# All eight pairs of weight tiles in Strassen's scheme, and a new order of work, in an attention and feed-forward kernel on one core

## The chip, the core and the metric

The program runs on one core of a Trainium2 chip, in one launch. The metric is the device time of that launch in microseconds (us), smaller being better. TensorE (PE) multiplies matrices, VectorE (DVE), ScalarE (ACT) and GpSimd (POOL) do elementwise work, SyncE (SP) issues the transfers. All five run side by side and wait for one another through semaphores; each works through its own list in order.

## The reference

Attention with positive random features for 8 batches of 8 heads (576 tokens, 64 channels a head, 128 features), and then a feed-forward layer on the 4,608 tokens x 512 channels that it gives:

```python
q_p, k_p = phi(q_s), phi(k_s)          # exp features, 128 a head
kv = einsum('bhsm,bhsd->bhmd', k_p, v)
num = einsum('bhsm,bhmd->bhsd', q_p, kv)
den = einsum('bhsm,bhm->bhs', q_p, k_p.sum(2))[..., None] + 1e-06
x = (num / den) as 4608 tokens x 512
h = x @ w_in                           # 512 -> 2048
g = maximum(h, 0) + log1p(exp(-abs(h)))
out = g @ w_out                        # 2048 -> 512
```

## The kernel before

**The arithmetic.** Each fp32 number is kept as a high part (fp32r, cut by a copy) and a low part (the rest, by a subtraction), and each product of the two layers is three matmuls: high x high, high x low, low x high. The weights are 16 tiles of 128 hidden columns (`fc` 0 to 15). Layer 1 of one tile on 512 tokens is 4 channel blocks x 3 = 12 matmuls of 128x512, made in two halves of six. Layer 2 of one tile is four steps (`tt` 0 to 3, 128 tokens each) of three matmuls, added up over the 16 tiles in an `acc` bank of PSUM. Between the two stands softplus: Abs, Exp and Ln on ACT, a max and add on DVE, a high copy on ACT or DVE, a low subtraction on DVE or POOL.

**The blocks.** Tokens go in two blocks of 256 and eight of 512. The last 64 tokens of each batch (the "rest") have no place in their batch's block: they are saved to DRAM as they come (`plan_save`), and together they are the last block, t8, loaded back by `plan_rest` in two transfers. The block before it is t7. Both are made together in `plan_both`.

**Strassen's scheme.** `plan_both` multiplies t7 and t8 by the weights in pairs of tiles (fa, fb). For a pair that is a product of 2x2 blocks: two token blocks, two halves of the channels, two weight tiles; done plainly, eight products of six matmuls (`plan_plain`). `plan_pair` makes it in seven products `p1` to `p7` of six matmuls, from sums of weight blocks (128x256; nine sums, and the cutting of four of them into high and low parts) and sums of token blocks (128x512, `plan_sums`, once for each of two channel blocks c, for all pairs), and adds the products up with five operations on DVE. `PLAIN = 1` makes the first pair plainly and seven by the scheme. With `plan_sums` the sum `first` takes the place of t8's own first half of the channels in `xh`, `xl`, so it waits for the plain pair (`plains`).

**The order.** Nothing is scheduled when the kernel is built: all steps are put in a list of works, and `ORDER` is a written-out list of them (entry = 2 x number of the work + which of its engines makes it). Each engine gets its works in that order. `in_order` gives each work a buffer when its turn comes (`take`, the one that came free earliest) and returns it (`give`) at its last use; a work waits for the last user of its buffer. `timed` reckons the times again, and `with_fill` puts idle matmuls (`fill`, L1775) where it reckons a gap of PE that is long enough.

**Names below.** "xp" is the product that gives x for a part of a batch (`plan_x`, L1183); "l1" and "l2" are steps of layers 1 and 2 of the block before t7; "L2" those of t7 and then t8; "P1.p5" is product 5 of pair 1.

Of the kernel before, what the change touches and what calls it, by code (L numbers as in the profile page):

```python
# [11 lines left out]
F32R = mybir.dt.float32r  # L12
# [25 lines left out]
COLD, LAG = 2.6, 1.85  # L38
# [5 lines left out]
PLAIN = 1  # L44
# [418 lines left out]
def favor_softplus_kernel(ctx, tc, q0, k0, qx, kx, tx, vv, om, wi, wo, out):  # L463
# [894 lines left out]
    def plan_both(i, box):  # L1358
# [84 lines left out]
        def plan_sums(c):  # L1443
# [5 lines left out]
            def third(i):  # L1449
                for k in range(3 if not i else 0):  # L1450
                    b[k] = at.tile([P, 2, n], F32R, name=f"x{k + 2}_{c}", tag=b["s", k], bufs=1)
                    b["f", k] = temp(b["t", k], n, f"xf{k}_{c}")
# [432 lines left out]
```

## Time and profile before

| | |
|---|---|
| time, median of 3 runs (from, to) | 977.64 us (977.54 to 988.13) |
| the profiled execution: its own time | 976.84 us |
| its span, first to last instruction | 975.1 us |
| busy: PE, DVE, ACT, POOL | 964.5, 790.5, 675.5, 283.9 us |
| PE matmuls | 5,511 |
| chain that ended last, by engine | PE 92%, DVE 5%, ACT 2%, issue 1%, DMA 1% |
| granted clock of PE | 1.0 |

The span is what the profiler sees between the first and the last instruction; the rest of the time lies around it. A matmul's duration is modelled and longer than its step: 128x512 matmuls show some 390 ns and follow each other every 0.23 us. So the busy time of PE hides gaps under about 0.16 us, and a stall is read from the distance of two starts.

### The profile page before, as it was taken

How to read it: one execution, taken by the hardware profiler on the slowest of the kernel's cores; microseconds unless marked ns; L12 is line 12 of the kernel's file. 1: busy time of each engine (PE TensorE's matmuls, PEld its weight loads, DVE VectorE, ACT ScalarE, POOL GpSimd, SP SyncE). 2: the span in 40 equal slices, each digit the busy share in tenths (PEclk: the TensorE clock that was granted, in tenths of full speed). 3: DMA queues.
4: the chain of work that ended last, by engine and by line, in shares of the span. 5: the costliest groups of instructions: out<-in, count | busy, mean ns of one | idle time of the engine just before them, and what ended most of it. 6: DMA issues, size and time to landing. Idle time of an engine off the chain costs nothing.

```text
span 975.1 us, 17613 instructions
## 1 busy us (share of the span) xinstructions
PE 964.5 (99%) x5511; PEld 791.1 (81%) x5511; DVE 790.5 (81%) x2774; ACT 675.5 (69%) x1668; POOL 283.9 (29%) x262
## 2 busy tenths in 40 slices
PE   8999999999999999999999999999999999999998
PEld 7878888888888878887888878887888777788887
DVE  8999988888978888888887878778887868999720
ACT  7999977768576876778695867677575536776510
POOL 1444442323245341034234343233223411200100
PEclk9999999999999999999999999999999999999999
DMA  9967355343423434532433244234431331000011
GB/s 339 363 237 248 111 164 149 108 136 117 131 82 93 130 110 121 157 120 79 130 125 120 81 126 139 66 109 124 139 119 38 99 124 44 1 1 1 1 43 44
DMA packets 65116, 113.85 MB, mean 117 GB/s; under 512 B 18376, under 2 KB 38016, under 8 KB 65024
## 3 DMA queue, kind: packets, MB, share of 16 engines
q1 hardware_dynamic: 64720, 112.54, 36.4%
q8 instruction: 44, 0.72, 0.3%
q14 instruction: 48, 0.39, 0.1%
q10 hardware_dynamic: 304, 0.20, 0.1%
HBM read 85.68 MB, written 27.03 MB: 116 GB/s over the span
## 4 chain that ended last, share of the span: by engine, by line
PE 92%; DVE 5%; ACT 2%; issue 1%; DMA 1%; SPq 0%; DVEq 0%; ACTq 0%
PE acc L1314 14%; PE acc L1315 13%; PE acc L1316 13%; PE h L1254 10%; PE h L1255 10%; PE h L1256 10%; PE xp L1183 3%; PE pb L1593 3%; PE ppk L714 3%; PE ppq L714 2%; PE pc L1593 2%; PE kt L855 2%; PE pa L1593 2%; PE ku L855 1%; PE ppk L689 1%
## 5 line engine op out<-in xcount | busy, mean ns | idle before, releaser
L1314 PE MATMUL acc<-wo,gh 128*128 128x512 f32 x512 | 204.2, 399 | 0.0
L1315 PE MATMUL acc<-wo,gh 128*128 128x512 f32 x512 | 200.7, 392 | 0.0
L1316 PE MATMUL acc<-wo,gl 128*128 128x512 f32 x512 | 199.5, 390 | 0.0
L1254 PE MATMUL h<-xh,wi 128*128 128x512 f32 (+1 forms) x512 | 189.0, 369 | 0.0
L1255 PE MATMUL h<-xl,wi 128*128 128x512 f32 (+1 forms) x512 | 186.4, 364 | 0.0
L1256 PE MATMUL h<-xh,wi 128*128 128x512 f32 (+1 forms) x512 | 185.7, 363 | 0.0
L1277 POOL TENSOR_TENSOR gl<-u,gh 128x512 fp32r<-128x512 f32 (+1 forms) x72 | 84.7, 1177 | 215.4 <-ACT gh L1273 137.7
L1260 ACT ACTIVATE u<-h 128x512 f32<-128x512 f32 (+1 forms) x128 | 70.5, 550 | 68.9 <-PE h L1256 55.8
L1314 PEld LDWEIGHTS acc<-wo,gh 128*128 128x128 f32 x512 | 96.3, 188 | 22.0 <-issue 6.4
L1316 PEld LDWEIGHTS acc<-wo,gl 128*128 128x128 f32 x512 | 96.2, 188 | 21.0
L1254 PEld LDWEIGHTS h<-xh,wi 128*128 128x128 f32 x512 | 96.4, 188 | 18.8 <-DVE u L1269 1.6
L1256 PEld LDWEIGHTS h<-xh,wi 128*128 128x128 f32 x512 | 96.5, 188 | 15.6
L1315 PEld LDWEIGHTS acc<-wo,gh 128*128 128x128 f32 x512 | 96.6, 189 | 14.3
L1255 PEld LDWEIGHTS h<-xl,wi 128*128 128x128 f32 x512 | 96.7, 189 | 13.5
L1269 DVE SCALAR_TENSOR_TENSOR u<-h,u 128x512 f32<-128x512 f32 (+1 forms) x128 | 78.8, 618 | 15.7 <-ACT u L1266 14.9
L1263 ACT ACTIVATE u<-u 128x512 f32<-128x512 f32 (+1 forms) x128 | 75.2, 587 | 1.9
L1266 ACT ACTIVATE u<-u 128x512 f32<-128x512 f32 (+1 forms) x128 | 74.6, 584 | 1.8
L1092 DVE CUSTOM_DVE_ANT_0 junk<-phq,zb 128x128 uint8<-128x128 f32 (+1 forms) x228 | 70.7, 341 | 3.7 <-ACT phq L734 2.3
L734 ACT ACTIVATE phk<-phk,smk 128x128 f32<-128x128 f32 x208 | 69.4, 393 | 5.0 <-DVE smk L749 4.7
L729 DVE CUSTOM_DVE_ANT_0 phk<-ppk,phk 128x128 f32<-128x128 f32 x208 | 51.5, 286 | 23.8 <-ACT phk L724 22.8
L734 ACT ACTIVATE phq<-phq,smq 128x128 f32<-128x128 f32 x194 | 62.2, 391 | 8.8 <-DVE smq L749 8.6
L1101 POOL TENSOR_TENSOR phq<-phq,dnq 128x512 f32<-128x512 f32 x37 | 42.2, 1144 | 89.2 <-DVE dnq L1097 87.7
(222 smaller groups left out, 1999.0 us busy)
## 6 DMA issues: line engine op xcount, KB each, us to landing
xk<-kx SPq DMA_DIRECT2D x28, 512.0 KB, 3.6
xq<-qx SPq DMA_DIRECT2D x28, 512.0 KB, 3.6
fdq<-flq SPq DMA_DIRECT2D x28, 512.0 KB, 3.0
qq<-fdq SPq DMA_DIRECT2D x112, 128.0 KB, 3.0
rawi<-wi SPq DMA_DIRECT2D x16, 512.0 KB, 8.1
rawo<-wo SPq DMA_DIRECT2D x16, 512.0 KB, 6.5
out<-o SPq DMA_DIRECT2D x32, 256.0 KB, 2.1
v<-vv SPq DMA_DIRECT2D x14, 576.0 KB, 5.0
```

The costliest lines, as they stand in the source:

```text
L734: nc.scalar.activation(x, x, AF.Exp, bias=b["sm"][:, 2, c : c + 1])
L1092: nc.vector.tensor_tensor_reduce(jk[r, k], ph[r, c], q.zb[r, h], 1.0, 1e-6, ALU.mult, ALU.add, dn[r, 0, c : c + 1])
L1254: nc.tensor.matmul(b["h"], wh, xh[:, cc, t], start=cc == 0, stop=False)
L1255: nc.tensor.matmul(b["h"], wh, xl[:, cc, t], start=False, stop=False)
L1256: nc.tensor.matmul(b["h"], wl, xh[:, cc, t], start=False, stop=cc == NCC - 1)
L1263: nc.scalar.activation(b["u"], b["u"], AF.Exp, scale=-1.0)
L1266: nc.scalar.activation(b["u"], b["u"], AF.Ln, bias=1.0)
L1269: nc.vector.scalar_tensor_tensor(b["u"], b["h"], 0.0, b["u"], ALU.max, ALU.add)
L1277: (nc.vector if e == "DVE" else nc.gpsimd).tensor_tensor(b["gl"], b["u"], b["gh"].bitcast(F32), ALU.subtract)
L1314: nc.tensor.matmul(dst, gh, w2[fc][:, 0, c], start=start, stop=False, **kw)
L1315: nc.tensor.matmul(dst, gh, w2[fc][:, 1, c], start=False, stop=False, **kw)
L1316: nc.tensor.matmul(dst, gl, w2[fc][:, 0, c], start=False, stop=stop, **kw)
```

## The change

- `PLAIN` goes from 1 to 0: the first pair is made by the scheme too. `plan_plain` is not called.
- `plan_sums`: the sums take their buffers when each is first written, no longer all at the first; each sum waits only for what it reads, so `first` no longer waits for both steps of the sum ahead of it. The high part of `first` waits for the old readers of its place (`old_reads`), there being no plain pair.
- `plan_rest`: the first of the two loads (channel blocks 0 and 1) is no longer cut into high and low parts, since only the sums read it.
- `LAG`, a constant of the planner's reckoning of transfers in the first 8 us, goes from 1.85 to 1.6. It can change the count of idle matmuls.
- `ORDER` is new from its entry 2,602 on (of 4,980 before and 4,998 after); the entries ahead of it are the same.

```diff
-COLD, LAG = 2.6, 1.85
+COLD, LAG = 2.6, 1.6
-PLAIN = 1
+PLAIN = 0
...
             def third(i):
-                for k in range(3 if not i else 0):
-                    b[k] = at.tile([P, 2, n], F32R, name=f"x{k + 2}_{c}", tag=b["s", k], bufs=1)
-                    b["f", k] = temp(b["t", k], n, f"xf{k}_{c}")
+                if not i:
+                    b["f", 1] = temp(b["t", 1], n, f"xf1_{c}")
...
             def high(k):
+                b[k] = at.tile([P, 2, n], F32R, name=f"x{k + 2}_{c}", tag=b["s", k], bufs=1)
                 act_high(b[k][:, 0], b["f", k])
...
-            a = ready[t7][c] + ready[t8][c] + ready[t7][c + 2] + ready[t8][c + 2]
-            t = do("DVE", dve(n), lambda: third(0), after=a, take=[("sx", b, ("s", k)) for k in range(3)] + [("hk", b, ("t", k)) for k in range(3)], port=True)
-            t = do("DVE", dve(n), lambda: third(1), after=[t], port=True)
+            t = do("DVE", dve(n), lambda: third(0), after=ready[t7][c] + [rests[0]["l"]], take=[("hk", b, ("t", 1))], port=True)
+            t0, t = t, do("DVE", dve(n), lambda: third(1), after=[t], port=True)
             w = do(
-                "DVE", dve(n), first, after=[t] + done_first, port=True, give=[(x, "x") for x in rests] if c else [],
+                "DVE", dve(n), first, after=[t0, rests[1]["l"]] + done_first, port=True, take=[("hk", b, ("t", 0))], give=[(x, "x") for x in rests] if c else [],
             )
...
-            h = do("ACT", copied(n), first_high, after=[w] + plains)
+            h = do("ACT", copied(n), first_high, after=[w] + old_reads(t8, n))
...
-            s4 = do("DVE", dve(n), lambda: fourth(0), after=[s2], port=True)
+            s4 = do("DVE", dve(n), lambda: fourth(0), after=[s2] + ready[t7][c + 2], port=True, take=[("hk", b, ("t", 2))])
...
-                h = do("ACT", copied(n), lambda k=k: high(k), after=[x])
+                h = do("ACT", copied(n), lambda k=k: high(k), after=[x], take=[("sx", b, ("s", k))])
...
             for p in range(2):
+                if not i:
+                    x_lows[t0, n, p] = l
+                    continue
```

Decoded, the two lists of PE from the last xp on (products of a pair by number; l2 of the last tiles):

```
before: xp, 8 plain halves among l2 13,2 to 14,3, l2 15,0 to 15,3, L2 0,0, P2.p1, L2 0,1-2, P1.p1, L2 0,3 1,0, P1.p2,
        L2 1,1-2, P2.p2, P1.p5, L2 1,3, P1.p6, ...
after:  xp, l2 10,2-3, l1 14, l2 11,0-3, l1 15, l2 12,0 to 15,0, P0.p1, l2 15,1-2, P0.p2, P1.p1, P0.p5, l2 15,3, P1.p5,
        P0.p6, L2 0,0-1, P0.p7, L2 0,2-3, P0.p3, P0.p4, P1.p6, P2.p1, P1.p2, ...
```

Works of DVE and POOL from `plan_rest` on, counted in the two lists (DVE's copies of outputs and its high copies are the same in both):

| | DVE 128x256 | DVE 128x512 | POOL 128x256 | POOL 128x512 |
|---|---|---|---|---|
| before | 82 | 121 | 9 | 6 |
| after | 88 | 118 | 16 | 10 |

## Rows read from the trace of the kernel before

**Rows 1.** The page, busy time, share of the span and instructions of PE and others.
```profile
PE 964.5 (99%) x5511; PEld 791.1 (81%) x5511; DVE 790.5 (81%) x2774; ACT 675.5 (69%) x1668; POOL 283.9 (29%) x262
```

**Rows 2.** Timeline of PE at its three stalls: start, duration, line, [idle before, releaser].
```profile
585.06 0.47 PE L714 MATMUL ppq<-omr,spq 128*128 128x256 f32 x2 [0.66 <-DVE smq L729]
...
821.06 0.39 PE L1316 MATMUL acc<-wo,gl 128*128 128x512 f32 x1
822.26 0.50 PE L1593 MATMUL pa<-xh,wi 128*128 128x512 f32 x1 [0.81 <-ACT ha L1619]
...
834.25 0.50 PE L1593 MATMUL pb<-xh,t 128*128 128x512 f32 x1 [0.82 <-DVE hc L1626]
```

**Rows 3.** The chain that ended last, in order of time: start, length, what.
```profile
819.53 2.00 DMA out<-o
821.63 0.59 ACT ha L1619
...
832.07 1.52 DVE tf L1516
...
847.55 1.36 PE pc L1593 x6
```

**Rows 4.** Groups of instructions by line and form, 780 us to the end: the plain pair.
```profile
L1429 PE MATMUL h<-xh,wi 128*128 128x512 f32 x16 | 6.4, 397 | 0.0
```

**Rows 5.** Timeline of PE, SP, DVE and ACT from the last xp on.
```profile
796.09 1.30 PE L1183 MATMUL xp<-qq,kvs 128*64 128x320 f32 x8
...
797.95 0.38 SPq L614 DMA_DIRECT2D rest<-r  x1
798.43 1.56 SPq L1695 DMA_DIRECT2D back<-rest  x2
...
802.37 1.50 DVE L1702 CAST xh<-back 128x512 fp32r<-128x512 f32 x1 [2.21 <-DMA back<-rest]
...
804.37 0.62 ACT L1702 CAST xh<-back 128x512 fp32r<-128x512 f32 x1 [1.20 <-DMA back<-rest]
```

**Rows 6.** DVE's pace on 128x512 and 128x256 (timeline), and an ACT group.
```profile
809.20 0.68 DVE L1478 TENSOR_TENSOR x<-xf,x 128x512 fp32r<-128x512 f32 x1
809.80 0.68 DVE L1395 SCALAR_TENSOR_TENSOR u<-h,u 128x512 f32<-128x512 f32 x1
...
863.66 0.42 DVE L1542 TENSOR_TENSOR t<-tf,t 128x256 fp32r<-128x256 f32 x1
864.00 0.42 DVE L1544 TENSOR_TENSOR t<-tf,t 128x256 fp32r<-128x256 f32 x1
...
L1372 ACT CAST t<-tf 128x256 fp32r<-128x256 f32 x21 | 8.2, 397 | 6.1 <-PE pb L1593 4.7 <-DVE tf L1530 0.8 <-DVE tf L1526 0.4
```

**Rows 7.** POOL: two groups by form, two of its timeline, and DVE beside one.
```profile
L1408 POOL TENSOR_TENSOR gl<-u,gh 128x512 fp32r<-128x512 f32 x3 | 4.2, 1397 | 78.2 <-DVE gh L1403 71.9 <-ACT gh L1403 6.3
...
L1544 POOL TENSOR_TENSOR t<-tf,t 128x256 fp32r<-128x256 f32 x4 | 2.9, 741 | 10.8 <-DVE xf L1472 8.2 <-ACT t L1372 2.5
...
832.03 1.28 POOL L1408 TENSOR_TENSOR g<-u,g 128x512 fp32r<-128x512 f32 x1 [5.01 <-ACT g L1403]
...
837.55 1.44 POOL L1544 TENSOR_TENSOR t<-tf,t 128x256 fp32r<-128x256 f32 x2
...
837.93 0.68 DVE L1630 TENSOR_TENSOR ha<-pb,ha 128x512 f32<-128x512 f32 x1
```

**Rows 8.** Windows: length, then busy time (count) of PE, PEld, DVE, ACT, POOL; clock, DMA share, GB/s.
```profile
451.20:785.00 333.80, 333.14 (x1812) 269.72 (x1812) 271.63 (x1086) 230.80 (x561) 110.99 (x99) 1.00 0.36 110
...
796.10:927.60 131.50, 129.87 (x573) 106.31 (x573) 112.50 (x216) 86.55 (x165) 14.39 (x14) 1.00 0.05 17
...
840.00:900.00 60.00, 60.00 (x267) 49.62 (x266) 56.50 (x119) 44.78 (x86) 1.96 (x2) 1.00 0.00 1
```

**Rows 9.** Timeline of PE: the idle matmuls near the start, and the last matmul.
```profile
7.90 0.68 PE L1775 MATMUL fill<-ident 128*128 128x128 f32 x4 [0.47 <-issue]
...
971.14 0.28 PE L1316 MATMUL right<-wo,g 128*128 128x256 f32 x1
```

More of the change, by code (lines that the diff above doesn't have):

```diff
@@ L1456, in first @@
             def first():
-                x, y, z = (b["f", k] for k in range(3))
+                x = b["f", 0] = temp(b["t", 0], n, f"xf0_{c}")
                 ve(x, rests[0]["t"][:, c], rests[1]["t"][:, c], add)
@@ L1470, in fourth @@
             def fourth(i):
+                if not i:
+                    b["f", 2] = temp(b["t", 2], n, f"xf2_{c}")
                 x, z = b["f", 0], b["f", 2]
@@ L1700, in plan_rest @@
             for p in range(2):
+                if not i:
+                    x_lows[t0, n, p] = l
+                    continue
                 def high(e, x=(slice(None), 2 * i + p, t), p=p, b=b):
```

253 rows, old and new, of the table ORDER are left out of this document.

## The prediction

> **What bounds the kernel now.** The page comes first: PE is busy 964.5 us, 99% of the span, and no other engine is over 81% [rows 1]. Then the timeline of PE is searched for places where two matmuls start further apart than the 0.23 us of the steady pace. From 451 us on (where the new list begins; found by counting layer-2 steps, 227 of them in the common part) there are three worth the name, with idle times of 0.66, 0.81 and 0.82 us [rows 2]. Start to start the middle one is 822.26 - 821.06 = 1.20 us, 0.97 over the pace, which is the idle time and 0.16 us of the last matmul's modelled tail; so the three are 0.81 + 0.97 + 0.98 = 2.77 us. The chain of waits says what was late at the two in the end stretch: ScalarE's copy of P1's first product, behind a 2.00 us store of an output whose buffer it wanted, and a 1.52 us VectorE sum [rows 3]. All else is PE's own work, so the time moves by matmuls taken out and by stalls that come or go. The profiled execution took 976.84 us; the median of the runs is 0.80 above it. Sums are made on the former, and 0.80 is added.
>
> **The change part by part.**
>
> *The matmuls.* The plain pair is 8 halves of six matmuls (48 of them; its first line shows 16 [rows 4]), the pair by the scheme 7 products of six. One product of six takes 1.36 us on the chain [rows 3]. PE's list is shorter by one such step and otherwise holds the same ones: 5,511 - 6 = 5,505 matmuls, -1.36 us. All of it lies on the path, since PE is the path; only a stall can take it back.
>
> *The extra sums.* P0 costs 9 weight sums, 4 low parts and 5 final sums. But part of the low parts goes from VectorE to POOL and the rests of channels 0 and 1 aren't cut any more, so by the counts in the two lists VectorE has 6 more steps on 128x256 and 3 fewer on 128x512. Its pace is 0.34 and 0.60 us [rows 6]: +2.0 - 1.8 = +0.2 us. ScalarE has five steps more, under 3 us beside 131.5 - 86.6 = 45 us of free time in the stretch [rows 8]. Both hidden: 0.
>
> *Attention must end sooner.* From the start of the last xp to the first L2 of t8 PE now has 1.23 + 22 x 0.68 (l2) + 4 x 1.36 (l1) + 56 x 1.36 + 64 x 0.68 = 141.3 us, against 131.5 before [rows 8]. So the last xp must come 9.8 us sooner. VectorE was idle 333.8 - 271.6 = 62 us from 451 to 785 us [rows 8], so the room is there; 4 to 5 us of its softplus work also moves behind xp. The 0.81 us stall of that part [rows 2] may go or come again in a new place: 0 to 2 us, and I take 0.8, what it is now.
>
> *The seam between xp and the sums.* Here the plain pair was the cover: eight halves, 10.9 us. In its place stand l2 and l1 steps that were made ahead of xp. With the last xp's start as 0, P0.p5, the first product to read a token sum, is at 1.23 + 21 x 0.68 + 4 x 1.36 + 3 x 1.36 = 25.0 us, P1.p5 at 27.1, P0.p6 at 28.4. What they wait for: the save of the rest starts at 1.9 us, the two loads at 2.3 us, and their first readers at 6.3 and 8.3 us [rows 5]; those are well ahead. ScalarE's cuts into t8's place wait for the last l1 of the block before (10.8 us), so the sums run from there on a VectorE that also makes two tiles' softplus. In its new list stands the copy of the first output bank, which can't start before l2 15,0 is done: 1.23 + 19 x 0.68 + 4 x 1.36 = 19.6, with some 0.2 us until the copy. From 19.8, thirteen steps lie up to P1's sum for p5 (8 x 0.34 + 5 x 0.60 = 5.7): 25.5. ScalarE's cut (0.40 [rows 6]) and POOL's low part (0.74 [rows 7]) make it 26.6, against 27.1. For P0.p6 five more VectorE steps follow, 2.7 us: 28.3 against 28.4. No slack is left, and two POOL steps stand in this stretch. A POOL step can hold VectorE up: a 128x256 sum took 1.52 us from 832.07 [rows 3], right behind POOL's start at 832.03 [rows 7], where 0.42 is usual [rows 6]. Two such, 1.1 us each, are 2.2 us. So this costs 0 to 2.0, and I take 1.0, the middle, since not every POOL step does it (the sum at 837.93, which reads PSUM, kept its 0.68 beside one [rows 7]). And four output tiles, three buffers of t7's P0 sums and three token sums share the same few buffers, as at 821 us: 0 to 1.0, by that stall; I take 0.6. Together 1.6 us.
>
> *The pairs behind it.* The 0.98 us stall at 834 us is of the old seam and goes. From 835 us to the end PE had no stall, with VectorE busy 56.5 of 60 us from 840 to 900 us [rows 8]. With more POOL steps: 0 to 2, I take 0.4.
>
> *LAG and the tail.* Fewer idle matmuls near the start can free up to 0.68 us [rows 9]; the chain there runs through transfers and ScalarE, so 0. The last steps (L2 of t8, ending at 971.14 [rows 9]) are in the same order: 0.
>
> *The sum.* -1.36 - 2.77 + 0.8 + 1.6 + 0.4 = -1.33. Execution profiled: 976.84 - 1.33 = 975.5; with 0.80, **976.3 us**.
>
> *A rule against the change.* POOL's groups show 0.74 us for a 128x256 step and 1.40 for a 128x512 one [rows 7]; with 7 and 4 more steps POOL works some 11 us more in the end stretch. The Trainium skill, in "SBUF — State Buffer" (section "SBUF: two separate sides"), says that VectorE, in an operation with two SBUF inputs, and GpSimd hold one pair of ports by an exclusive lock, for the whole instruction, and that the loser blocks fully. By that rule nearly all of the 11 us would be VectorE's loss; by the rows alone, the share that happens to meet. The trace agrees, with 1.52 in place of 0.42 us, and also with a PSUM reader left alone. What it would do to the time is the first rival.
>
> **The rivals.**
>
> *POOL's steps block VectorE, and PE starves between the pairs (slower).* In P1 to P7 the moved steps relieve VectorE of 7 x 0.34 + 4 x 0.60 = 4.8 us and block it for 7 x 0.74 + 4 x 1.40 = 10.8 us: 6 us lost. It decides from the point where the loss in the dense stretch is over the 3.5 us that VectorE was idle there [rows 8]. 2.5 to 6 us of stalls in place of my 0.4 give 978.4 to 981.9 us. For it: VectorE is at 94% there. Against it: 9.8 us more of PE work stand between xp and t8's L2, and POOL was idle for most of that time, so that the new steps can lie under PSUM readers. Chance 0.15.
>
> *Attention isn't done in time.* If the last xp can't move up by the 9.8 us, PE waits for it, in one piece or in several small ones in the stretch from 451 us. Every stall of that kind adds to the time; 2 to 5 us give 977.5 to 980.5. Against it: 62 us of idle VectorE. Chance 0.12.
>
> *No stalls at all.* The seam and the stretches around it hold, and the old stalls go: -1.36 - 2.77, or 973.5, and up to 975 with a small one left. For it: PE showed only three stalls in 520 us, so an order without any is near. Against it: the seam's arithmetic has no slack. Chance 0.2.
>
> *The change doesn't do what it says:* the new list would have to hold plain steps or as many products; counted, it holds 56 products and no plain half. That is no case.
>
> **How the numbers follow.** The forecast, 975 to 978 us, gets 0.5; no stalls 0.2; POOL 0.15; attention 0.12; and 0.03 stays for a new wait that repeats over the whole second half. The range reaches from the no-stall case to inside both slow ones: 973.5 to 979.6. Its ends are also those of the terms: all zero, 973.5; seam 3, the others 1 each, 978.5, and some more. 2% are 19.6 us, about what a measurement of this kernel can tell from no change, and more than any term here: within 2% 0.97. Slower by more needs a wait of 1 us in twenty places: 0.02. Faster by more would need PE work to vanish: 0.01.
>
> **What the changed kernel's profile would show.** 336 matmuls of the products' line and none of the plain pair's; some 5,505 in all, fewer if idle ones go. The step of six at 1.36 us as before. The stalls at 585, 821 and 834 us gone, and in their place a wait of P1.p5 or P0.p6 for POOL's or VectorE's low part some 27 us behind the last xp, which itself starts near 785 us. VectorE as busy as before in the end stretch, POOL near 26 us there instead of 14.4. If PE shows no stall from 785 us on, the seam was priced too high; if it shows several among P2 to P7 behind stretched VectorE sums, the first rival holds. What would make the prediction wrong altogether is a stall of several us ahead of the last xp.

## The result and the profile after

The changed kernel takes 986.13 us (median of 22 runs, 975.40 to 989.71), the kernel before 977.66 us (22 runs, 976.70 to 988.13). The ratio is 1.0065, with a 95% interval of 1.0039 to 1.0091 (the medians alone: 1.0087): slower, by less than 2%, and outside the range of 973.5 to 979.6 us. The runs of the changed kernel fall in two groups, three at 975.4 to 976.2 us, where the forecast was, and nineteen at 984.5 to 989.7; of the 22 of the kernel before two are at 988.1. The profiled execution (986.19 us) is of the upper group.

The page of the changed kernel, busy time and count of PE and others, to be read beside [rows 1]; the count is 5,501, which is 5,511 less the six matmuls of the forecast and less the four idle ones of [rows 9]:

```profile
PE 976.2 (99%) x5501; PEld 802.6 (82%) x5501; DVE 785.8 (80%) x2762; ACT 680.8 (69%) x1685; POOL 302.9 (31%) x276
```

PE is busy to the end, and yet the time is longer. So the two kernels are first compared at a place that both share. The list is the same up to its entry 2,602, so the first product xp stands in both behind the same work, but for idle matmuls. The timeline of PE there, of the kernel before and then of the changed one:

```profile
102.35 1.08 PE L1183 MATMUL xp<-qq,kvs 128*64 128x256 f32 x8
```

```profile
113.46 1.08 PE L1184 MATMUL xp<-qq,kvs 128*64 128x256 f32 x8
```

11.11 us are lost ahead of anything that the new order touches. From there to the start of the last matmul, 979.74 in the changed kernel and 971.14 before [rows 9], it is 866.28 against 868.79 us: 2.51 us won. So the question is the first 100 us. Timeline of PE from the start, changed kernel:

```profile
1.05 2.50 PE L1781 MATMUL fill<-idle 128*128 128x128 f32 x10 [1.05 <-DVE marks L506]
3.78 1.22 PE L690 MATMUL ppk<-omf,xk 64*128 64x128 f32 x8 [0.23 <-DVE omf L502]
5.70 6.22 PE L690 MATMUL ppk<-omf,xk 64*128 64x128 f32 x40 [0.69 <-DMA xk<-k]
...
13.74 1.23 PE L690 MATMUL ppk<-omf,xk 64*128 64x128 f32 x8
```

and of the kernel before:

```profile
3.72 1.23 PE L689 MATMUL ppk<-omf,xk 64*128 64x128 f32 x8 [0.16 <-DVE omf L501]
5.43 1.99 PE L689 MATMUL ppk<-omf,xk 64*128 64x128 f32 x24 [0.48 <-DMA xk<-k]
...
8.64 0.78 PE L689 MATMUL ppk<-omf,xk 64*128 64x128 f32 x8
```

Eight ppk matmuls (products of k with the feature matrix) take 1.23 us in the changed kernel, still at 13.74, and 0.78 us at 8.64 in the kernel before: the same instructions at TensorE's two levels, 1.2 and 2.4 GHz. In the kernel before the pace has changed by 5.43 us, where 24 take 1.99 us. (The forty in one line show that PE had no gap while it made them.) The four `fill<-ident` matmuls of [rows 9], at 7.90 us, are not there any more in the changed kernel. How long that lasts is told by the groups of PE by line and form, 12 to 35 us, before and then changed (mean ns of one is the last number ahead of the second bar):

```profile
L906 PE MATMUL kt<-xk 128*128 128x65 f32 x56 | 7.4, 276 | 0.0
```

```profile
L907 PE MATMUL kt<-xk 128*128 128x65 f32 x56 | 13.5, 419 | 0.0
```

and by the windows of PE (length, busy, count, clock, DMA share, GB/s), before and then changed:

```profile
12.00:35.00 23.00, 22.24 (x212) 1.00 1.04 400
```

```profile
12.00:35.00 23.00, 23.00 (x128) 1.00 1.04 401
```

128 matmuls in place of 212, with PE busy all the time. The clock's column misleads here: the trace's record of the clock begins with its first change, which is the rise to 2.4 GHz, at 37.27 us in the changed kernel and at 5.09 us before; until then the column shows 1.00 whatever the level. Durations and counts show it.

The end stretch is to be read beside [rows 2]. Timeline of PE at all of its waits of 0.15 us or more from 451 us on:

```profile
820.38 0.39 PE L1595 MATMUL pc<-xl,wi 128*128 128x512 f32 x1
820.76 0.73 PE L1595 MATMUL pc<-xh,wi 128*128 128x512 f32 x2
...
824.33 0.40 PE L1317 MATMUL acc<-wo,gl 128*128 128x512 f32 x1
825.10 1.65 PE L1595 MATMUL pb<-x,t 128*128 128x512 f32 x6 [0.38 <-DVE hb L1624]
...
827.74 0.39 PE L1317 MATMUL acc<-wo,gl 128*128 128x512 f32 x1
828.26 1.66 PE L1595 MATMUL pc<-x,wi 128*128 128x512 f32 x6
...
833.61 0.93 PE L1595 MATMUL pa<-xh,wi 128*128 128x512 f32 x2
```

Start to start, less 0.23 us a matmul: 0.15 (P1.p5), 0.54 (P0.p7), 0.29 (P0.p3) and 0.20 us (P1.p2, the second matmul of the last line, which the chain of waits below starts at 834.04), 1.2 in all. The old ones of [rows 2] are gone, and behind 835 us there is none. The largest of the new ones, on the chain of waits (beside [rows 3]):

```profile
821.67 0.38 ACT o L1332
822.07 2.16 DMA out<-o
824.36 0.70 DVE hb L1624
825.10 1.66 PE pb L1595 x6
...
834.04 1.66 PE pa L1595 x6
```

This is the stall of 821 us in a new place: a store of 2.16 us holds the buffer that the sum `hb` wants. POOL holds VectorE up in this stretch, and behind it VectorE holds POOL up (timeline of POOL, then of VectorE; beside [rows 7]):

```profile
814.52 1.01 POOL L1546 TENSOR_TENSOR t<-tf,t 128x256 fp32r<-128x256 f32 x1 [16.98 <-ACT t L1373]
...
840.43 1.02 POOL L1546 TENSOR_TENSOR t<-tf,t 128x256 fp32r<-128x256 f32 x1 [12.55 <-ACT t L1373]
```

```profile
814.86 0.96 DVE L1514 TENSOR_TENSOR tf<-wi,wi 128x256 f32<-128x256 f32 x1
...
816.34 0.41 DVE L1514 TENSOR_TENSOR tf<-wi,wi 128x256 f32<-128x256 f32 x1
...
840.17 0.69 DVE L1396 SCALAR_TENSOR_TENSOR u<-hc,u 128x512 f32<-128x512 f32 x1
840.96 0.69 DVE L1628 TENSOR_TENSOR hc<-pb,ha 128x512 f32<-128x512 f32 x1
```

At 814.86 VectorE's step takes 0.96 us in place of 0.41; at 840.43 it is POOL's that takes 1.02 in place of 0.74, and VectorE's keep their 0.69. In the dense stretch VectorE has become freer, 51.63 us busy of 60 (the same stretch of work as the last window of [rows 8], where it had 56.50), and POOL 13.81 in place of 1.96:

```profile
848.00:908.00 60.00, 60.00 (x266) 49.72 (x266) 51.63 (x100) 40.93 (x78) 13.81 (x14) 1.00 0.00 1
```

One part of the gain is lost behind the last matmul. From its start to the end of the span it was 3.9 us (971.14 to 975.1) and is 4.7 (979.74 to 984.4). Timeline of VectorE and ScalarE there, before:

```profile
970.45 0.42 DVE L1326 COPY o<-acc 128x256 f32<-128x256 f32 x1 [0.72 <-PE acc L1316]
...
967.26 0.37 ACT L1331 COPY o<-acc 128x256 f32<-128x256 f32 x1 [16.24 <-PE acc L1316]
969.76 0.37 ACT L1331 COPY o<-acc 128x256 f32<-128x256 f32 x1 [2.13 <-DVE o L1326]
```

and changed:

```profile
979.38 0.42 DVE L1327 COPY o<-acc 128x256 f32<-128x256 f32 x1 [1.05 <-ACT o L1332]
...
978.98 0.65 ACT L1332 COPY o<-acc 128x256 f32<-128x256 f32 x2 [16.25 <-PE acc L1317]
```

ScalarE's first copy of the last tile (`p` in `plan_out`) started 3.88 us ahead of the last matmul and now starts 0.76 ahead; the other ScalarE copy stands right behind it, and VectorE's copy waits for `p`.

### The profile page after: what moved, and what is told of

It is laid out like the page before. It is cut to its first block, busy times and chain, and to the rows that moved or that the text cites. A ratio compares the mean times of both kernels' runs of the same rounds, so it can differ in the third digit from the quotient of the medians.

```text
span 984.4 us, 17655 instructions
## 1 busy us (share of the span) xinstructions
PE 976.2 (99%) x5501; PEld 802.6 (82%) x5501; DVE 785.8 (80%) x2762; ACT 680.8 (69%) x1685; POOL 302.9 (31%) x276
## 4 chain that ended last, share of the span: by engine, by line
PE 92%; DVE 5%; ACT 1%; issue 1%; DMA 1%; SPq 0%; DVEq 0%; ACTq 0%
PE acc L1315 13%; PE acc L1316 13%; PE acc L1317 13%; PE h L1255 10%; PE h L1256 10%; PE h L1257 10%; PE pb L1595 3%; PE xp L1184 3%; PE ppk L715 3%; PE ppq L715 2%; PE pc L1595 2%; PE pa L1595 2%; PE kt L856 2%; PE ppk L690 2%; PE kt L907 1%; PE ku L856 1%
## 5 line engine op out<-in xcount | busy, mean ns | idle before, releaser
L1317 PE MATMUL acc<-wo,gl 128*128 128x512 f32 x512 | 199.8, 390 | 0.0
L1278 POOL TENSOR_TENSOR gl<-u,gh 128x512 fp32r<-128x512 f32 (+1 forms) x74 | 87.1, 1178 | 215.4 <-ACT gh L1274 136.4
L1317 PEld LDWEIGHTS acc<-wo,gl 128*128 128x128 f32 x512 | 96.3, 188 | 20.8
L1102 POOL TENSOR_TENSOR phq<-phq,dnq 128x512 f32<-128x512 f32 (+1 forms) x39 | 42.2, 1089 | 81.8 <-DVE dnq L1098 70.0
```

The costliest lines, as they stand in the source:

```text
L1278: (nc.vector if e == "DVE" else nc.gpsimd).tensor_tensor(b["gl"], b["u"], b["gh"].bitcast(F32), ALU.subtract)
L1317: nc.tensor.matmul(dst, gl, w2[fc][:, 0, c], start=False, stop=stop, **kw)
```

## The experiments

Theory 1 is that without the four idle matmuls TensorE's clock rises late. Theory 2 is chance, whatever the list. Theory 3 is another effect: of `LAG`, by its choice of buffers (first form), or of the new order (second form).

**Idle matmuls back, in the changed kernel: as they were, and twice as many.**

```diff
-COLD, LAG = 2.6, 1.6
+COLD, LAG = 2.6, 1.85
# second kernel, besides:
-                all_.append((emit, names[0], n))
+                all_.append((emit, names[0], 2 * n))
```

> The changed kernel with LAG put back from 1.6 to 1.85, and nothing else: its plan then places the idle matmuls behind the fourth PE step again (two calls, four records), as the kernel before does. Theory 1 (the four idle matmuls that went with LAG 1.6 were what brought TensorE's clock from 1.2 to 2.4 GHz early): most executions at 975 to 977 us, ratio to the kernel before about 0.998, and the profiled execution shows the first layer's ppk groups of eight at 0.78 us from about 8.6 us on, not at 1.23 us. Theory 2 (the start of the clock is chance of the execution, whatever the list): the times stay mixed as those of the changed kernel, median 984 to 987 us. Theory 3 (LAG's other effects, or the new second half of the list, cost the time): 984 to 987 us for the second half; if it is LAG by its choice of buffers, 975 to 977 us here, and the third kernel of this call tells that from theory 1.

> The changed kernel with LAG 1.85 and twice as many idle matmuls behind the fourth PE step (four calls, eight records). Theory 1: as the first kernel of this call, 975 to 977 us, with at most 0.7 us more where they don't hide, and as many or more of the executions in the lower group. Theory 2: mixed, median 984 to 987 us. Theory 3 (second half of the list): 984 to 987 us.

Measured: 976.62 us (12 runs, 976.04 to 979.56), ratio to the kernel before 0.9991 (0.9983 to 1.0); and 976.61 us (12 runs, 975.55 to 980.36), 0.9987 (0.9975 to 0.9999). No run above 981 us. In the profiled executions the clock rises at 4.85 and at 9.47 us. Theory 1 stands; the new order, theory 3's second form, is out.

**Idle matmuls out, in the kernel before: by LAG, and by leaving them out alone.**

```diff
-COLD, LAG = 2.6, 1.85
+COLD, LAG = 2.6, 1.6
# the other kernel, LAG as before:
-        for w in with_fill(out_, held, room["any"], 1e9, fill):
+        for w in with_fill(out_, held, room["any"], 0, fill):
```

> The kernel before with LAG 1.6 in place of 1.85 and nothing else: no idle matmuls behind the fourth PE step any more, the plain pair and the old order kept. Theory 1 (idle matmuls): 985 to 990 us in most executions, ratio 1.008 to 1.012, ppk groups of eight at 1.23 us until some 25 to 37 us. Theory 2 (chance of the execution): as the kernel before, 976.7 to 978.4 in most. Theory 3: by LAG's choice of buffers 985 to 990, by the new second half 977.6.

> The kernel before with LAG 1.85 and all its buffers chosen as before, but the planner is not allowed to place the idle matmuls behind the fourth PE step (four records fewer). Theory 1: 985 to 990 us in most executions, as the second kernel of this call; ppk groups of eight at 1.23 us until 25 to 37 us. Theory 2 and both forms of theory 3: 976.7 to 978.4 us, as the kernel before.

Measured: 986.54 us (6 runs: one at 977.75, five at 986.2 to 988.0), 1.0075 (1.0047 to 1.0103); and 988.18 us (4 runs, 987.98 to 991.22), 1.0111 (1.0094 to 1.0127). So the four idle matmuls are enough to explain the loss, with nothing of the new order in the kernel. The profiled execution with LAG 1.6 is the one at 977.75, and it is useful: from the first xp (103.26) to the last matmul (972.04) it takes 868.78 us, the kernel before 868.79. Behind the first xp LAG does nothing else.

**The same four idle matmuls with 64 rows instead of 128.** In the changed kernel with LAG 1.85:

```diff
-    def fill(tag, n, idle=ident):
+    def fill(tag, n, idle=ident, rows=M // 2):
...
-            nc.tensor.matmul(t, idle, idle, start=True, stop=True)
+            nc.tensor.matmul(t, idle[:rows], idle[:rows], start=True, stop=True)
...
-        fill("at.0", 5, idle)
+        fill("at.0", 5, idle, P)
```

> The changed kernel with LAG 1.85 and the four idle matmuls behind the fourth PE step cut from 128 to 64 rows of the contraction, as the ppk matmuls around them have; same count, same columns. If any idle matmul there will do (it is the gap that counts): as the first experiment, 976 to 977 us in most executions. If it is their 128 rows that the ppk matmuls lack: as with none, 984 to 990 us in most.

Measured: 988.86 us (4 runs, 986.59 to 990.03), 1.0109 (1.0096 to 1.0122): as with none. Two timelines of PE are compared: first one with 128 rows, of an execution in which the clock was still low at the idle matmuls (the first kernel with POOL's two steps moved, below), then that of this kernel:

```profile
5.55 2.93 PE L690 MATMUL ppk<-omf,xk 64*128 64x128 f32 x24 [0.57 <-DMA xk<-k]
8.44 1.19 PE L1781 MATMUL fill<-ident 128*128 128x128 f32 x4
...
11.19 1.11 PE L907 MATMUL kt<-xk 128*128 128x65 f32 x8
```

```profile
5.98 2.93 PE L690 MATMUL ppk<-omf,xk 64*128 64x128 f32 x24 [0.93 <-DMA xk<-k]
8.87 1.19 PE L1781 MATMUL fill<-ident 64*128 64x128 f32 x4
...
12.20 1.11 PE L907 MATMUL kt<-xk 128*128 128x65 f32 x4
```

With four matmuls of 128 rows the clock rises at 9.73 us, and eight kt matmuls take 1.11 us; with four of 64 rows, as long and as many, 1.11 us holds four of them, and the rise comes at 39.32 us. In neither is there a gap ahead of the idle matmuls, so they don't work here by filling one.

**Fourteen idle matmuls at the very start instead of ten**, in three kernels: the changed one with LAG 1.85, the changed one as it is, and the kernel before.

```diff
-        fill("at.0", 5, idle)
+        fill("at.0", 7, idle)
```

> The changed kernel with LAG 1.85 and fourteen instead of ten idle matmuls at the very start. Theory 1, carried on (more such matmuls ahead of the first ppk group bring TensorE's clock up at about 5 us in every execution, not only in some): 975.0 to 976.3 us in most, the ppk groups of eight at 0.78 us or less from their second group on. Rival (the clock rises at about 9 us as with ten, and the first ppk group is only later): 976.5 to 977.5 us.

> The changed kernel with its own LAG of 1.6, so without the four idle matmuls behind the fourth PE step, and fourteen instead of ten at the start. If enough of them at the start bring TensorE's clock up before the first layer's matmuls begin, and those then hold it: 975.5 to 976.5 us in most executions. If the four behind the fourth step are needed whatever comes before: 984 to 990 us in most.

> The kernel before with fourteen instead of ten idle matmuls at the start and nothing else. It gives the changed order's own worth at the same start: the forecast's sum (matmuls, stalls) says 1.3 us more than the changed kernel with the same start (976.3), so 977.6 us; the two traces' common marker says 2.4 us more, so 978.7. If the fourteen bring the clock up earlier than in the kernel before, 0 to 1 us less than either.

Measured, in this order: 976.33 us (11 runs, 975.71 to 976.60), 0.9985 (0.9976 to 0.9993); 981.59 us (12 runs: six at 976.0 to 978.5, six at 984.7 to 989.5), 1.0038 (1.0006 to 1.0069); 977.51 us (12 runs, 977.18 to 977.84), 0.9996 (0.9988 to 1.0005). Fourteen at the start and the four behind the fourth step give the early clock in every run; fourteen without the four in half of them. How it is lost is seen in the second one's profiled execution, timeline of PE and then its windows:

```profile
8.06 0.46 PE L690 MATMUL ppk<-omf,xk 64*128 64x128 f32 x2 [0.49 <-DVE smk L745]
8.82 1.12 PE L690 MATMUL ppk<-omf,xk 64*128 64x128 f32 x8 [0.30 <-ACT xk L758]
10.15 0.71 PE L690 MATMUL ppk<-omf,xk 64*128 64x128 f32 x6 [0.22 <-ACT xk L758]
```

```profile
5.00:11.00 6.00, 4.74 (x48) 1.00 1.04 393
12.00:35.00 23.00, 23.00 (x129) 0.50 1.04 401
```

Here the record holds both changes: the clock rises at 4.78 us, PE makes 64-row matmuls with waits of 0.49, 0.30 and 0.22 us between them, and at 11.61 us the clock falls to 1.2 GHz, where it stays until 35.50.

A run's mean granted clock tells the two ways of losing apart: as the record begins with the first change, a late first rise leaves the mean at 0.999 or 1.0, and this execution, with its fall, has 0.988. Of the changed kernel's nineteen long runs twelve have 0.999 or 1.0, and seven, at 984.5 to 985.1 us, have 0.987. Of the five long ones of the kernel before with LAG 1.6, four have 0.987 or 0.988; where the idle matmuls alone were left out, all four have 1.0. So the four idle matmuls do two things: they bring the clock up where the start has missed it (at 9.73 us above), and with them a fall behind an early rise is rare. It isn't excluded: among 35 runs of the kernel before that were taken beside these, one has 988.53 us and 0.988. Nor is the early rise sure with them: by the same sign, one of the eleven runs of the first kernel with POOL's two steps moved (below) missed it, with 990.91 us and 0.999. That it is the waits which bring the clock down is not shown, for the profiled execution of the kernel before with LAG 1.6 had a longer one and kept 2.4 GHz from 5.09 us on:

```profile
8.70 0.90 PE L689 MATMUL ppk<-omf,xk 64*128 64x128 f32 x8 [1.05 <-DVE smk L744]
```

The first and the third kernel have the same start, and compare the two orders: 976.33 - 977.51 = -1.18 us. They ran on different chips; each against the kernel before beside it (977.80 and 977.67), they are 1.47 and 0.16 us faster, so the new order is worth 1.2 to 1.3 us.

**The seam: POOL's two steps given to VectorE.** First in the changed kernel with LAG 1.85:

```diff
 ORDER: works 4423 (low part of a P0 sum) and 4469 (first low part of P1)
-    ... 8847 ... 8939 ...
+    ... 8846 ... 8938 ...
```

> The changed kernel with LAG 1.85 (the first experiment's kernel) and the two POOL steps of the seam, the low part of P0's sum and the first low part of P1, given to VectorE at the same places of the list. Theory A (the seam's stalls come of POOL holding VectorE up, as the prediction priced 1.0 us of it): the first 128x256 weight sum of P1 takes 0.41 instead of 0.96 us, the stalls between 815 and 835 us fall from about 1.2 us to 0.6 or less, and the time by 0.4 to 0.7 us. Rival B (they come of buffers and stores and of VectorE's own list): the stalls stay at 1.0 to 1.4 us, or grow by up to 0.8, since VectorE gets two steps of 0.42 us more; time 976.4 to 977.4 us.

Measured: 977.46 us (11 runs, 977.06 to 978.02 and one at 990.91), 1.0007 (0.9984 to 1.003). It tells nothing clean: the planner now reckoned a gap ahead of the seam and put twelve idle matmuls there (809.80 to 811.30 us). So once more, with fourteen at the start and none allowed behind 100 us:

```diff
-        fill("at.0", 5, idle)
+        fill("at.0", 7, idle)
...
-        for w in with_fill(out_, held, room["any"], 1e9, fill):
+        for w in with_fill(out_, held, room["any"], 100, fill):
```

> The kernel with fourteen idle matmuls at the start (LAG 1.85) and the two POOL steps of the seam given to VectorE, with idle matmuls kept out of everything behind the first 100 us (the planner had put twelve of them ahead of the seam when those steps were moved before). Theory A (POOL's hold on VectorE makes part of the seam's stalls): the stall of P0.p6 behind hb, about 0.6 us, shrinks or goes, the seam's sum falls from about 1.3 us to 0.7, and the time from 976.3 to about 975.7 us. Rival B (buffers, stores and VectorE's own list make them): the sum stays at 1.2 to 1.5 us or grows, 976.3 to 977 us.

(The stall behind `hb` is at P0.p7; "P0.p6" in that text is a slip.) Measured: 977.13 us (12 runs, 976.87 to 979.04), 0.9995 (0.9986 to 1.0003), 0.80 us more than with POOL's steps (976.33; 0.9 more when each is taken against the kernel before beside it). The stretched VectorE step is gone, all are 0.41 to 0.42 us, and so is the wait behind `hb`, and yet P1.p5 waits longer than the whole seam did:

```profile
809.99 0.40 PE L1595 MATMUL pc<-xl,wi 128*128 128x512 f32 x1
812.39 0.73 PE L1595 MATMUL pc<-xh,wi 128*128 128x512 f32 x2 [2.01 <-DVE wi L1524]
```

VectorE makes that low part only at 811.92, in its turn; POOL had made it from 809.80 to 810.60 in the kernel with the same start. Neither theory A nor theory B holds as it was put: POOL's steps hold VectorE up by half a microsecond and are still worth it, since VectorE's list is full there.

**All sixteen low parts of weights that POOL makes from the seam on, given to VectorE**: in the kernel with LAG 1.85 as first, and then with fourteen idle matmuls at the start and none behind 100 us:

```diff
 ORDER, each entry less one:
-    8847, 8939, 8959, 9059, 9063, 9175, 9275, 9279, 9283, 9371, 9479, 9495, 9499, 9587, 9599, 9607
+    8846, 8938, 8958, 9058, 9062, 9174, 9274, 9278, 9282, 9370, 9478, 9494, 9498, 9586, 9598, 9606
```

> The changed kernel with LAG 1.85 and all sixteen low parts of weights that POOL makes in the end stretch given to VectorE at the same places of the list; POOL keeps only the low parts and adds of softplus there. Prediction's first rival (POOL's steps block VectorE for longer than they relieve it): VectorE loses 16 x 0.34 = 5.4 us and gets back up to 16 x 0.74; no new stalls, time 975.5 to 976.6 us. The prediction's own view (POOL's steps lie mostly under work that doesn't meet them, and relieve VectorE): stalls of 1 to 5 us behind 835 us in several of the pairs, time 977.5 to 981 us.

> As the kernel before this one, with all sixteen low parts of weights of the end stretch on VectorE, and no idle matmuls behind the first 100 us. If POOL's steps cost more than they relieve (the prediction's first rival), 975.3 to 976 us. If they are under cover, as the prediction took it, the time is that of the two-step version or up to 1 us more.

Measured: the first got twelve idle matmuls ahead of the seam too, 977.62 us (12 runs, 976.82 to 981.40), 1.0003 (0.9993 to 1.0012). The second: 978.68 us (12 runs, 976.74 to 981.51), 0.9998 (0.9978 to 1.0018). Its profiled execution has a wait of 1.29 us for `spq` at 263.5 us, in the part that no edit touches, and at the seam 1.86 us where the two-step version had 2.01; behind 830 us it has no wait. So in the profiled executions the fourteen steps behind the seam make no wait on PE, wherever they are made: POOL's hold on VectorE decides nothing there, and neither does its relief. The median can't be set against the two-step version's: four runs are at 976.7 to 977.4 us, like its 977.13, but seven are at 978.5 to 981.5 with a granted clock of 0.998, as in the mid-run fall told of at the end. Why these came so often with this list is open.

**The end: `p` put back to where the kernel before has it.** Kernel with LAG 1.85 and fourteen at the start; t7's last ScalarE copy (9830) moves with it, to stay ahead:

```diff
-    ... 9828, 9948, 9950, ... 9962, 9830, 9964, 9986, 9980, ...
+    ... 9828, 9948, 9830, 9986, 9950, ... 9962, 9964, 9980, ...
```

> The kernel with LAG 1.85 and fourteen idle matmuls at the start, and ScalarE's copy p of the last output tile moved in the list from behind L2 15,3 of its left half to right behind L2 12,3, as the list of the kernel before has it (t7's last ScalarE copy goes with it, so that it stays ahead of p). If p stood too late in the list (it waits for the left half's matmuls, which are issued ahead of it, and the last copies queue up behind it): from the start of the last matmul to the end of the span 3.9 us, as in the kernel before, not 4.6; time 975.6 us in place of 976.3. If the last stores set the end, however the copies are ordered: 4.6 us and 976.3 us.

Measured: 975.46 us (10 runs, 975.13 to 978.17), ratio to the kernel before 0.9978 (0.9969 to 0.9988). Timeline of ScalarE and VectorE:

```profile
965.73 0.37 ACT L1332 COPY o<-acc 128x256 f32<-128x256 f32 x1 [13.49 <-PE acc L1317]
968.23 0.37 ACT L1332 COPY o<-acc 128x256 f32<-128x256 f32 x1 [2.13 <-DVE o L1327]
...
968.91 0.42 DVE L1327 COPY o<-acc 128x256 f32<-128x256 f32 x1 [0.72 <-PE acc L1317]
```

The last matmul starts at 969.60, the span ends at 973.5: 3.9 us, as before the change. In the list of the change `p` comes behind the matmuls of the left half of its bank, and waits for them (PE acc L1317, in the changed kernel's row). This version beats both kernels, the one before by 2.3 us or 0.2%.

## Why the prediction was wrong, and where it was right

The step that failed is the first sentence of "LAG and the tail": fewer idle matmuls "can free up to 0.68 us; the chain there runs through transfers and ScalarE, so 0". It priced the idle matmuls as the time that they take, and not by what they do to the clock of the matmuls around them. In truth their going cost 8.8 us in the median (986.54 for the kernel before with LAG 1.6, against 977.78 for the kernel before beside it), and 10.4 where they alone were left out (988.18). The reason given for the 0 fails with it: at 1.2 GHz PE had no gap from 5.70 to 37.27 us, so in that stretch PE itself was the path, and not transfers and ScalarE. The profile of before shows half of this: the pace of ppk goes from 1.23 us for eight at 3.72 us to 1.99 for 24 at 5.43, so the clock starts low. It doesn't show what the four idle matmuls are for, since in that execution the clock had risen at 5.09 us, ahead of them; only runs without them do.

A passage of the Trainium skill would have warned, and misled in part: "TensorE: Matmul & The Clock Gate" (section "What's actually happening") has the clock set by how busy PE has lately been, and the point of its rise differ from run to run. The second half agrees in kind with the two groups of runs of one list. The first half, taken as the profile's busy share, does not: 23.00 us busy of 23.00 at 1.2 GHz, in the changed kernel.

The other terms, by the traces:

- *The matmuls, -1.36.* Right: six fewer, and the four idle ones besides.
- *Three old stalls, -2.77.* Right: none is left in its place.
- *The stall ahead of the last xp, +0.8.* Did not come: 0. Attention was done in time; that rival falls. The last xp came 12 us sooner ahead of the last matmul, more than the 9.8 asked for: 979.74 - 792.64 = 187.10 us, against 971.14 - 796.09 = 175.05.
- *The seam, +1.6.* 1.2 us in the changed kernel (1.4 in the one with fourteen idle matmuls), at P1.p5, P0.p7, P0.p3 and P1.p2; the buffers' part was put at 0.6, the stall behind the store is 0.54. POOL's part was overpriced as a loss: moving its steps made it worse.
- *The pairs behind it, +0.4.* 0. The rival in which POOL blocks VectorE falls too: with the added steps on either engine PE has no wait there, and VectorE was freer than before. The rule that stood behind it, that the loser of the two waits for the whole instruction, is seen from both sides at 814.86 and 840.43; behind the seam it costs PE nothing.
- *The tail, 0.* "In the same order" holds for PE alone. ScalarE's copy `p` had moved: +0.7 us in the profiled spans, shown by putting it back (976.33 to 975.46).

From the first xp to the last matmul the sum of these was -1.33 and the two kernels with the same start give 866.70 (103.17 to 969.87) less 868.73 (103.08 to 971.81), -2.03; with the tail's 0.7 on top, -1.2 in spans (974.5 and 975.7) and -1.2 to -1.3 in medians. The terms as measured, -1.36 - 2.77 + 1.4, make -2.7, so 0.7 us more was lost between the first xp and the last matmul in gaps too small to be listed. The near hit of -1.33 is in part luck: the 0.8 and 0.4 that did not come and the 0.2 too much for the seam cancel against the tail's 0.7 and these 0.7, which were not priced. Where the clock is early, the forecast of 976.3 us is nearly met: 975.4 to 976.2 in the changed kernel's three such runs.

What stays open: why executions of one list differ, so that without the four idle matmuls the clock is early and stays up in three runs of 22. No run here could choose it.

## What to carry to other kernels

Count what a matmul without a use does to the clock of its neighbours before counting its own time: here 0.7 us of idle matmuls were worth 9. When a constant of a planner changes, list every instruction that comes or goes by it and price the stretch around each. And when a search reorders a list, compare every engine's last steps, not only those of the bound one.

## What the runs showed of the hardware that was not expected

PE was busy without a gap for over 30 us at 1.2 GHz, in the changed kernel from 5.70 to 37.27 us: with ppk and ppq matmuls of 64 rows, kt of 65 columns and a few others. The clock also falls in mid-run: in the changed kernel with LAG 1.85 PE waited 0.33 and 1.29 us for `spq` at 262 to 263.7 us, and fell to half for 3.41 us from 264.26 on (windows of PE):

```profile
264.30:267.60 3.30, 3.30 (x11) 0.50 0.63 176
```

That execution took 979.56 us against a median of 976.62: with 1.6 us of waits, 2.9 us more. It doesn't always follow: in the profiled execution with sixteen low parts moved and fourteen idle matmuls at the start, the same wait of 1.29 us left the clock at 2.4 GHz.
